# A second staging buffer for layer 0's weights, and nine bias tiles instead of ten

## The chip, the cores and the metric

The kernel runs on one core of a Trainium2 chip. The metric is the device time of one execution, in microseconds (us); the median of the runs counts. A core has TensorE (matmuls, with a queue of its own for weight loads, PEld in the profile), VectorE (DVE), ScalarE (ACT), GpSimd (POOL) and SyncE (SP), which here only issues DMAs. Each engine runs its instructions in the order of its queue; an instruction that waits holds up all that stand behind it on that engine.

## What is computed

Attention with a learned position bias, and two feed-forward layers on its output. With four batches, eight heads, 576 positions and head width 64 (2304 tokens of width 512; the hidden width of the layers is 2048):

```python
scores = scale * np.matmul(q, k.transpose(0, 1, 3, 2))
x = (psi_rel / psi_i)[..., None]
bias = np.maximum(x @ w1 + b1, 0.0) @ w2
scores = scores + bias.transpose(2, 0, 1)[None]
attn = softmax(scores)
x = (attn @ v).transpose(0, 2, 1, 3).reshape(2304, 512)
h = x @ w_in0                        # layer 0
x = (h * np.cos(h)) @ w_out0
h = x @ w_in1                        # layer 1
out = (np.maximum(h, 0) + alpha * np.minimum(h, 0)) @ w_out1
```

The feed-forward weights come in double precision; the kernel reads them as pairs of 32-bit words. Every operand of a large matmul is split into a high and a low part, and three products stand for one.

## The kernel before

**Stages.** `bias_phase` builds the bias rows in DRAM (36 groups of 16 positions). Then `attention` goes through 16 pairs of two heads and one batch: the bias belongs to the heads, so four pairs (the four batches) share one set of rows, and pair n uses set n // 4. `h_phase0` and `o_phase(0)` are layer 0, `h_phase1` and `o_phase(1)` layer 1. TensorE's part of layer 0 begins while the last pair still ends.

**A pair of attention.** Each pair has five score stages: stage 0 for the last 64 positions of both heads, stages 1 to 4 for 128 positions of each head. From pair 4 on they go in the order 1, 0, 2, 3, 4. For a stage TensorE makes the scores S (line 476), VectorE adds the bias and takes the extreme in one instruction (line 492: `P` from `S` and the bias tile `bt`, and `nm`), and ScalarE takes the exp (line 505). Then TensorE transposes the result (T_A, T_B, L_A, L_B, Tr; ScalarE and VectorE copy them out of PSUM, lines 555 and 557), GpSimd spreads the reciprocal sums (rb, line 517) and TensorE multiplies with v into x_A and x_B (lines 592, 595). The result xe goes to DRAM on SP's queue (line 613). Queries and keys of later pairs are loaded on SP and split by GpSimd (qh, kh, ql, kl; lines 454, 459).

**Bias tiles.** `load_bias` (lines 414 to 427) loads one tile of 128 x 576 for each of the nine (stage, head) parts of a set, on SP. The tiles come from the ring `bt_p` with BTB = 10 tiles. The load for the next set is written right behind the maximum of the set's last pair that reads the old part: in pairs 3, 7 and 11. A tile can be loaded once the maximum that reads its former content is done.

**Staging.** While attention runs, the weights of layer 0 are prepared piece by piece. `conv` turns a double-precision block into single precision: two ScalarE instructions (`wc`, `wp`, lines 225 and 226), two on VectorE (lines 231 and 232) and an add on GpSimd (line 235). `wi` then splits a block of w_in into a high part (a copy, GpSimd, line 314) and a low part (GpSimd, line 318). The first NDIR = 6 blocks stay on the chip; the ten others go into a tile with the tag `st` and from there to DRAM (line 321, SP, 512 KB). `stage_wo` does the same for pairs of blocks of w_out: sums and differences on VectorE (`wt`, tag `ct`, line 278), then `leave_w` for each of four groups: split by ScalarE (line 251) and GpSimd (line 253) into a tile of the tag `st` (named `sw`), and stores on SP (line 268, 256 KB each; one for the first group, two for the others). Five such pairs, k = 3 to 7, are staged in this way, the others in `h_phase0` without a store. `h_phase0` loads the staged weights back on SP. The tags `st` and `ct` belong to the pool `wt`, which has one buffer for each tag: a new `st` or `sw` tile can only be written when the store of the last one has landed.

**Order.** The order in which each engine runs all this is set by the Tile scheduler at build time, which places instructions by priority and by its own simulated times; stores and loads on SP are placed in the same way. On the chip every queue then keeps its order. The pieces of staging are written between the stages by `step`.

Of the kernel before, what the change touches and what calls it, by code (L numbers as in the profile page):

```python
# [10 lines left out]
F32R = mybir.dt.float32r  # L11
# [25 lines left out]
HP, LP, XP, CPRI, SP = 200, 0, 300, -50, 400  # L37
HIA, LOP = 2, 1
UPB, EPB = {"D": 11, "A": 4}, 6
PBUF, BTB = 6, 10  # L40
FIRST, SIDE, SMOD, BFIRST, BRATE, SPL, WS0, WSR, PER = 4, 6, 2, 8, 2.5, 3, 28, 3.2, 1.0
SR = 2.0
NSP = 2
# [29 lines left out]
def attn_mlp_kernel(ctx: ExitStack, tc: tile.TileContext, a: dict, out: bass.AP):  # L73
# [95 lines left out]
    wpool = {}  # L169
# [7 lines left out]
    cstack = ExitStack()  # L177
    rstack = ExitStack()
    astack = ExitStack()
    raws_w = {}  # L180
    pinned = []
    anchor = []
# [75 lines left out]
    def leave_w(layer, k, g, x):  # L258
        ps = GRPS[layer][g]
        n = len(ps)  # L260
        if (layer == 0 and k < NIP) or (layer == 1 and g < 3):
            w = WO[layer, g]
            yield from split_to(w[:, :, k, 0, :], w[:, :, k, 1, :], x)
            return
        st = wpool["t"].tile([128, 2, 2, 256], F32R, tag="st", name=f"sw{layer}_{k}_{g}")
        yield from split_to(st[:, 0:n, 0, :], st[:, 0:n, 1, :], x)
        for i, p in enumerate(ps):
            (ge if pinned else sy).dma_start(out=w2_d[layer][SLOT[p], :, k], in_=st[:, i].bitcast(F32))
        yield
# [31 lines left out]
    def wi(layer, f):  # L301
        box = []
        yield from conv(layer, f, 0, box)
        if layer:
            t = wt[f] = wpool["h"][(f + 1) % 4].tile([128, 2, 512], F32R, tag="w", name=f"v{f}")
        elif f < NDIR:
            t = wt[f] = wpool["a"].tile([128, 2, 512], F32R, tag="w", name=f"w{f}")
        else:
            t = wpool["t"].tile([128, 2, 2, 256], F32R, tag="st", name=f"st{f}").rearrange("p a b c -> p a (b c)")
        hi, lo = t[:, 0], t[:, 1]  # L310
        if layer:
            se.activation(out=hi, in_=box[0], func=AF.Copy)
        elif HIA == 2:
            keep(0, ge.tensor_copy(out=hi, in_=box[0]))
        else:
            keep(0, se.activation(out=hi, in_=box[0], func=AF.Copy))
        yield
        keep(1, (ve if layer else ge).tensor_tensor(out=lo, in0=box[0], in1=hi.bitcast(F32), op=ALU.subtract))
        yield
        if not layer and f >= NDIR:  # L320
            sy.dma_start(out=w_d[f], in_=t.bitcast(F32))
            yield
# [28 lines left out]
    def attention():  # L351
        with ExitStack() as c:
# [308 lines left out]
            def more_bias(g):  # L661
                nonlocal ng
                while ng < min(g, NG):
# [8 lines left out]
                    if ng == NG:  # L672
                        for _ in side:
                            pass
                        bstack.close()
                        right = dict(side="right", reuse_waits="tile")
                        wpool["s"] = rstack.enter_context(tc.tile_pool(name="ws", bufs=2, **right))
                        wpool["c"] = rstack.enter_context(tc.tile_pool(name="wc", bufs=2, **right))
                        wpool["t"] = astack.enter_context(tc.tile_pool(name="wt", bufs=1, **right))
                        wpool["a"] = astack.enter_context(tc.tile_pool(name="wa", bufs=NDIR, **right))  # L680
                        wpool["x"] = astack.enter_context(tc.tile_pool(name="xh0", bufs=NCC, **right))

            pend_exp = []
            fill = []
# [8 lines left out]
            while i < NS or pend_exp or waiting or fill:  # L693
                new = []
                if i < NS:
# [3 lines left out]
                    hp, b = pairs[n]  # L699
                    more_bias(max(BFIRST + int(BRATE * j), GNEED[s]))  # L700
                    for m in range(FIRST, NP):
                        f = pos[m, 1]
# [36 lines left out]
                else:  # L739
                    while fill and credit > 0:  # L740
                        d, fn, _ = fill.pop(0)
# [339 lines left out]
    def h_phase1():  # L1081
        runs = [[(0, 512), (512, 1024)], [(1024, 1536), (1536, 2048)], [(2048, 2304)]]
        with ExitStack() as c:
# [83 lines left out]
            step(1000)  # L1167

    attention()
    pinned.append(1)  # L1170
    h_phase0()
    astack.close()
# [70 lines left out]
```

## Time and profile before

| | us |
|---|---|
| median of three runs | 1102.74 |
| the three runs | 1100.99, 1102.74, 1106.53 |
| the profiled execution | 1098.82 |
| its span, first to last instruction | 1097.0 |
| TensorE busy | 1061.3 (97%) |
| VectorE busy | 807.9 (74%) |
| ScalarE busy | 643.9 (59%) |
| GpSimd busy | 254.4 (23%) |

The profile belongs to one execution. It gives the busy time of each engine, and each instruction's start, duration and the idle time of its engine before it, with what ended that idle time. Times in it count from the span's start. The end of a matmul is modelled from the next one's start, so that a TensorE that is shown as busy may still have waited for some tenths of a microsecond. The granted clock of TensorE is at its higher level (2.4 GHz) from 150 us on. The shares are means over stages with different limits: the bias rows until some 100 us, attention until 340, layer 0 until 713, layer 1 from there.

### The profile page before, as it was taken

The page shows a single profiled execution, that of the slowest core. Times are in us where ns is not written, and L with a number is a line of the kernel's source. Part 1 is how long each engine was busy: PE and PEld are TensorE (multiplying, and loading weights), DVE is VectorE, ACT ScalarE, POOL GpSimd, SP SyncE. Part 2 cuts the span into 40 slices and gives each one's busy share as a digit, 9 for nine tenths or more (in the row PEclk, how much of TensorE's full clock was granted, in tenths as well). Part 3 has the DMA queues.
Part 4 walks back from the last instruction along what each step waited for, and adds up shares of the span by engine and source line. Part 5 has one row for each costly group of instructions (what it writes and reads, how often), then busy time and mean ns, then how long its engine had stood idle before and what let it go on. Part 6 is the DMA issues. An engine that isn't in the chain of part 4 may idle for free.

```text
span 1097.0 us, 18821 instructions
## 1 busy us (share of the span) xinstructions
PE 1061.3 (97%) x7078; PEld 898.6 (82%) x7078; DVE 807.9 (74%) x1292; ACT 643.9 (59%) x1076; POOL 254.4 (23%) x248
## 2 busy tenths in 40 slices
PE   7689899999989999999999999999999999999998
PEld 2246677777767779888899999988888889999998
DVE  8886688777875888778787778668765847777673
ACT  6897688877885565545454454456555534444442
POOL 5405566756442220010000000423322300000000
PEclk9899999999999999999999999999999999999999
DMA  8765657666459673436568172876765649564621
GB/s 277 221 182 167 207 147 246 224 204 223 161 190 341 237 276 127 142 135 220 200 205 308 57 240 78 325 256 222 227 216 184 204 176 353 171 201 131 216 70 47
DMA packets 107595, 219.77 MB, mean 200 GB/s; under 512 B 11504, under 2 KB 57328, under 8 KB 106096
## 3 DMA queue, kind: packets, MB, share of 16 engines
q1 hardware_dynamic: 77104, 157.74, 45.1%
q10 hardware_dynamic: 27968, 50.34, 12.3%
q0 software_dynamic: 2432, 10.49, 2.5%
q8 instruction: 56, 0.92, 0.3%
q14 instruction: 35, 0.29, 0.1%
HBM read 133.98 MB, written 84.56 MB: 199 GB/s over the span
## 4 chain that ended last, share of the span: by engine, by line
PE 74%; DVE 6%; DMA 6%; ACT 3%; issue 2%; POOL 2%; SPq 0%; ACTq 0%; POOLq 0%; DVEq 0%
PE v L1138 18%; PE ob L1007 14%; PE h L804 10%; PE oc L1007 9%; PE oa L1007 9%; PE S L476 5%; PE x_B L595 2%; PE T_B L570 2%; PE T_A L570 2%; PE x_A L595 1%; DMA w_d<-sw 1%; DMA w<-w_d 1%; DMA xlo<-x_d 1%; DVE P L492 1%; DVE tb L815 1%
## 5 line engine op out<-in xcount | busy, mean ns | idle before, releaser
L1138 PE MATMUL v<-x,v 128*128 128x512 f32 (+1 forms) x984 | 198.0, 364 | 0.0
L1138 PEld LDWEIGHTS v<-x,v 128*128 128x128 f32 x984 | 168.5, 189 | 29.5
L804 PE MATMUL h<-xhi,w 128*128 128x512 f32 (+1 forms) x640 | 184.6, 372 | 0.8 <-PE h L804 0.4
L235 POOL TENSOR_TENSOR wc<-wc,wp 128x512 int32<-128x512 int32 x64 | 88.5, 1383 | 222.7 <-DVE wc L232 160.1
L804 PEld LDWEIGHTS h<-xhi,w 128*128 128x128 f32 x640 | 115.9, 188 | 24.1 <-PE h L804 1.9
L989 ACT ACTIVATE op<-a 128x768 fp32r<-128x768 f32 x84 | 70.5, 844 | 83.4 <-PE ob L1007 27.6
L804 PE MATMUL h<-xlo,w 128*128 128x512 f32 (+1 forms) x320 | 118.6, 371 | 0.0
L990 DVE TENSOR_TENSOR op<-a,op 128x768 fp32r<-128x768 f32 x84 | 80.1, 957 | 51.3 <-ACT op L989 49.1
L505 ACT ACTIVATE P<-P,nm 128x576 f32<-128x576 f32 x128 | 98.6, 772 | 21.7 <-DVE nm L492 21.5
L492 DVE CUSTOM_DVE_ANT_0 P<-S,bt 128x576 f32<-128x576 f32 x128 | 91.6, 751 | 24.6 <-PE S L476 16.6
L989 ACT ACTIVATE op<-b 128x768 fp32r<-128x768 f32 x84 | 70.7, 844 | 61.1 <-PE ob L1007 22.2
L990 DVE TENSOR_TENSOR op<-b,op 128x768 fp32r<-128x768 f32 x84 | 79.8, 955 | 27.4 <-ACT op L989 27.2
L1149 DVE SCALAR_TENSOR_TENSOR u<-v,asg,u 128x1024 f32<-128x1024 f32 (+2 forms) x48 | 48.0, 1013 | 41.2 <-ACT u L1148 40.9
L1007 PE MATMUL ob<-op,wo 128*128 128x384 f32 x432 | 76.4, 336 | 0.0
L1007 PEld LDWEIGHTS ob<-op,wo 128*128 128x128 f32 x432 | 75.1, 188 | 0.0
L804 PEld LDWEIGHTS h<-xlo,w 128*128 128x128 f32 x320 | 60.3, 189 | 10.9
L813 ACT ACTIVATE ta<-h,quart 128x1024 int32<-128x1024 f32 x36 | 39.9, 1109 | 48.2 <-PE h L804 27.4
L1148 ACT ACTIVATE u<-v,sgn 128x1024 f32<-128x1024 f32 (+2 forms) x48 | 43.0, 898 | 41.9 <-PE v L1138 41.8
L476 PE MATMUL S<-kh,qh 64*128 64x288 f32 (+1 forms) x270 | 53.4, 350 | 13.1 <-DVE nm L492 13.0
L814 DVE SCALAR_TENSOR_TENSOR tb<-ta,h 128x1024 f32<-128x1024 int32 x36 | 43.8, 1218 | 23.6 <-ACT ta L813 20.8
L817 ACT ACTIVATE tb<-tb,hpi 128x1024 f32<-128x1024 f32 x36 | 41.2, 1146 | 26.3 <-DVE tb L815 26.3
L136 DVE TENSOR_SCALAR u<-at,thr 128x576 f32<-128x576 f32 (+17 forms) x120 | 54.3, 522 | 2.1 <-PE bps L141 2.0
(154 smaller groups left out, 2142.6 us busy)
## 6 DMA issues: line engine op xcount, KB each, us to landing
a<-g_d SPq DMA_DIRECT2D x60, 384.0 KB, 4.7
g_d<-tb ACTq DMA_DIRECT2D x36, 512.0 KB, 3.2
b<-g_d SPq DMA_DIRECT2D x48, 384.0 KB, 4.6
raw<-in_wi_dram SPq DMA_DIRECT2D x32, 512.0 KB, 3.8
raw<-in_wo_dram SPq DMA_DIRECT2D x32, 512.0 KB, 3.9
g_d<-u ACTq DMA_DIRECT2D x28, 512.0 KB, 2.7
bias_d<-be SPq DMA_DIRECT2D x36, 295.5 KB, 3.5
w_d<-sw SPq DMA_DIRECT2D x35, 256.0 KB, 2.6
```

The costliest lines, as they stand in the source:

```text
L136: ve.tensor_scalar(u[:, 0:n], at[:, 0:n], thr[:, m:m + 1], None, op0=ALU.max)
L235: ge.tensor_tensor(out=c, in0=c, in1=p, op=ALU.add)
L476: pe(te.matmul(ps[:, hf, 0:HS], lhsT=w[r, 128 * i:128 * i + 128], rhs=m[r, c0:c0 + HS], start=(j == 0), stop=(j == len(terms) - 1)))
L492: keep(2, ve.tensor_tensor_reduce(out=sn.rearrange("p (a b) -> p a b", a=2), in0=ps[:, :, 0:HS], in1=bt[hp, s].rearrange("p (a b) -> p a b ...
L505: exps.append(se.activation(out=e, in_=e, func=AF.Exp, bias=nm, scale=-1.0, accum_out=sums[n, u][:, col, 0:1]))
L570: pe(te.transpose(out=ps[:, o:o + 128], in_=Pp[n, i][:, (S + 64) * h + 128 * cc:(S + 64) * h + 128 * cc + 128], identity=ident))
L804: te.matmul(ps[:, i], lhsT=w_[:, wx, w], rhs=xx[:, 0:n], start=(j == 0), stop=(j == 11))
L989: se.activation(out=o[:, 0], in_=x, func=AF.Copy)
L990: lows.append(ve.tensor_tensor(out=o[:, 1], in0=x, in1=o[:, 0].bitcast(F32), op=ALU.subtract))
L1007: ins = te.matmul(ps[:, m], lhsT=x[:, sl] if L else w[:, sl], rhs=w if L else x, start=first, stop=kk == NK - 1 and n == 2, skip_group_che ...
L1138: ins = te.matmul(both[:, i, 0:a1 - a0], lhsT=w[:, wx, 128 * cc:128 * cc + 128], rhs=x[:, xx, cc, a0 - o:a1 - o], start=(n == 0), stop=(n ...
L1149: ve.scalar_tensor_tensor(out=g, in0=ps, scalar=asg[:, f:f + 1], in1=g, op0=ALU.mult, op1=ALU.max)
```

## The change

The ring of bias tiles gets nine tiles instead of ten: as many as one set has parts, so that each part of the next set goes into a tile of which the same set still needs one. The tag `st` of layer 0 moves into a pool of its own, `wst`, with two buffers, opened behind the others on the right side and closed when `attention` has been written, before the pools of `h_phase0` are opened. `ct` stays in the old pool; layer 1's staging uses the old pool as before.

```diff
-PBUF, BTB = 6, 10
+PBUF, BTB = 6, 9
...
     astack = ExitStack()
+    sstack = ExitStack()
...
-        st = wpool["t"].tile([128, 2, 2, 256], F32R, tag="st", name=f"sw{layer}_{k}_{g}")
+        st = wpool["t" if pinned else "st"].tile([128, 2, 2, 256], F32R, tag="st", name=f"sw{layer}_{k}_{g}")
...
-            t = wpool["t"].tile([128, 2, 2, 256], F32R, tag="st", name=f"st{f}").rearrange("p a b c -> p a (b c)")
+            t = wpool["st"].tile([128, 2, 2, 256], F32R, tag="st", name=f"st{f}").rearrange("p a b c -> p a (b c)")
...
                         wpool["x"] = astack.enter_context(tc.tile_pool(name="xh0", bufs=NCC, **right))
+                        wpool["st"] = sstack.enter_context(tc.tile_pool(name="wst", bufs=2, **right))
...
     attention()
+    sstack.close()
     pinned.append(1)
```

No instruction of an engine is added or removed. TensorE's order stays but for two matmuls of layer 0. On the other engines the staging pieces move against those of attention. (Lines of the kernel after are one to three higher.)

GpSimd where pair 7 ends and pair 8 begins; stN is block N of w_in, rbN_A the spread sums of pair N. Before:

```order
L517 COPY rb6_B_2461<-sm6_B_2458 128x320
L459 TENSOR_TENSOR kl10_3050<-rk10_2914,kh10_3049 128x640
L318 TENSOR_TENSOR st7_2180<-wc0_7_0_2171,st7_2180 128x512
L789 TENSOR_TENSOR xlo0_1_4850<-xlo0_1_4850,xhi0_1_4859 128x512
L517 COPY rb7_A_2613<-sm7_A_2610 128x256
L314 CAST st8_2313<-wc0_8_0_2233 128x512
L235 TENSOR_TENSOR wc0_9_0_2378<-wc0_9_0_2378,wp0_9_0_2379 128x512
L454 CAST qh11_3297<-rq11_3169 128x640
L318 TENSOR_TENSOR st8_2313<-wc0_8_0_2233,st8_2313 128x512
```

After:

```order
L319 TENSOR_TENSOR st7_2183<-wc0_7_0_2174,st7_2183 128x512
L236 TENSOR_TENSOR wc0_8_0_2236<-wc0_8_0_2236,wp0_8_0_2237 128x512
L518 COPY rb6_B_2464<-sm6_B_2461 128x320
L460 TENSOR_TENSOR ql10_3050<-rq10_2916,qh10_3049 128x640
L460 TENSOR_TENSOR kl10_3053<-rk10_2917,kh10_3052 128x640
L791 TENSOR_TENSOR xlo0_1_4854<-xlo0_1_4854,xhi0_1_4863 128x512
L315 CAST st8_2316<-wc0_8_0_2236 128x512
L236 TENSOR_TENSOR wc0_9_0_2381<-wc0_9_0_2381,wp0_9_0_2382 128x512
L518 COPY rb7_A_2616<-sm7_A_2613 128x256
L319 TENSOR_TENSOR st8_2316<-wc0_8_0_2236,st8_2316 128x512
L315 CAST st9_2390<-wc0_9_0_2381 128x512
```

Block 7 is finished before pair 6's sums are spread instead of behind them, and block 9 is begun before pair 11's queries are split.

ScalarE in pair 13, from its first exp to the two of stage 2 (P13_1); sw0_k_g is group g of the k-th pair of w_out blocks. Before:

```order
L505 ACTIVATE P13_0_4007,sume3_119<-P13_0_4007,nm13_1_4008 128x576
L555 ACTIVATE T12_B_4026<-Tr12_4027 128x8x64
L505 ACTIVATE P13_0_4007,sume3_119<-P13_0_4007,nm13_5_4010 128x576
L555 ACTIVATE T12_B_4026<-T12_B_1_4062 128x2x256
L251 ACTIVATE sw0_3_1_3206<-wt0_3_3161 128x2x256
L225 ACTIVATE wc0_8_1_3343<-raw0_8_1_3091 128x512
L505 ACTIVATE Pr13_4058,sume4_120<-Pr13_4058,nm13_0_4059 128x576
L555 ACTIVATE T12_B_4026<-T12_B_3_4074 128x2x256
L505 ACTIVATE P13_1_4102,sume3_119<-P13_1_4102,nm13_2_4103 128x576
L505 ACTIVATE P13_1_4102,sume3_119<-P13_1_4102,nm13_6_4105 128x576
```

After:

```order
L506 ACTIVATE P13_0_4010,sume3_119<-P13_0_4010,nm13_1_4011 128x576
L227 ACTIVATE wp0_10_1_3685<-raw0_10_1_3414 128x512
L506 ACTIVATE P13_0_4010,sume3_119<-P13_0_4010,nm13_5_4013 128x576
L556 ACTIVATE T12_B_4029<-T12_B_1_4065 128x2x256
L506 ACTIVATE Pr13_4061,sume4_120<-Pr13_4061,nm13_0_4062 128x576
L556 ACTIVATE T12_B_4029<-T12_B_3_4077 128x2x256
L252 ACTIVATE sw0_4_1_3522<-wt0_4_3459 128x2x256
L226 ACTIVATE wc0_10_1_3684<-raw0_10_1_3414 128x512
L252 ACTIVATE sw0_4_2_3559<-wt0_4_3459 128x2x256
L506 ACTIVATE P13_1_4105,sume3_119<-P13_1_4105,nm13_2_4106 128x576
L506 ACTIVATE P13_1_4105,sume3_119<-P13_1_4105,nm13_6_4108 128x576
```

The staging is one pair of blocks further on at the same place, two groups are split one right behind the other, and in the whole of pair 13 ScalarE has 6 conversions and 6 splits instead of 3 and 3 (4 and 4 instead of 4 and 1 in pair 12, 5 and 5 instead of 3 and 4 in pair 14). From pair 15's first exp on, up to the last copy of a transposed tile, 5 conversions and splits remain instead of 10.

SP where the set of pairs 8 to 11 is loaded; btS_p is part p of set S. Before:

```order
L426 DMA bt1_4_1631<-bias_d_57 128x576
L433 DMA rq7_2136<-in_q_dram 128x640
L423 DMA bt1_8_1633<-bias_d_57 128x512
L424 DMA bt1_8_1633<-bias_d_57 128x64
L426 DMA bt2_1_2453<-bias_d_57 128x576
```

After:

```order
L322 DMA w_d_78<-st6_2073 128x1024
L190 DMA raw0_10_0_2385<-in_wi1_dram 128x1024
L427 DMA bt2_1_2456<-bias_d_57 128x576
L424 DMA bt2_5_2458<-bias_d_57 128x512
L425 DMA bt2_5_2458<-bias_d_57 128x64
L614 DMA x_d_58<-xe6_A_2487 128x256
L419 DMA bt2_0_2507<-bias_d_57 64x576
L322 DMA w_d_78<-st7_2183 128x1024
L419 DMA bt2_0_2507<-bias_d_57 64x576
```

The first part of a set moves from behind the last part of the set before (three pairs earlier) to the others of its own set; the store of block 7 now stands between two halves of a bias tile.

## Rows read from the trace of the kernel before

**Rows 1.** The page, part 1: busy us (share of the span) and instructions of each engine.

```profile
PE 1061.3 (97%) x7078; PEld 898.6 (82%) x7078; DVE 807.9 (74%) x1292; ACT 643.9 (59%) x1076; POOL 254.4 (23%) x248
```

**Rows 2.** Windows by pair: start:end, length, busy us (instructions) by engine, PEclk, DMA share, GB/s.

```profile
133.06:148.79 15.73, 15.64 (x145) 12.10 (x144) 12.33 (x32) 12.29 (x27) 11.73 (x13) 1.00 0.64 185
...
180.21:197.40 17.19, 16.37 (x145) 12.17 (x143) 11.38 (x31) 13.52 (x33) 12.08 (x13) 1.00 0.98 319
...
228.80:244.17 15.37, 15.37 (x143) 12.09 (x143) 12.47 (x33) 12.31 (x29) 6.70 (x8) 1.00 0.65 214
244.17:261.71 17.54, 16.38 (x144) 12.18 (x143) 11.31 (x31) 13.65 (x33) 13.11 (x14) 1.00 0.91 304
261.71:277.08 15.37, 15.37 (x143) 12.09 (x143) 13.29 (x34) 12.50 (x30) 8.10 (x9) 1.00 0.36 117
277.08:294.63 17.55, 16.14 (x145) 12.11 (x143) 14.04 (x36) 15.25 (x36) 6.60 (x8) 1.00 0.53 180
294.63:312.08 17.45, 15.73 (x143) 12.13 (x143) 13.24 (x36) 14.35 (x33) 7.45 (x8) 1.00 0.49 160
312.08:339.88 27.80, 26.02 (x199) 19.42 (x198) 17.16 (x39) 19.01 (x43) 11.73 (x12) 1.00 0.69 219
```

**Rows 3.** Waits, 120 to 340 us: in total, times, the longest.

```profile
POOL st L314 <- DMA w_d<-st: 19.5, 7, 5.1
...
ACT sw L251 <- DMA w_d<-sw: 9.1, 6, 3.9
```

**Rows 4.** Timeline of GpSimd: start, us, what [idle before it and what ended it].

```profile
192.17 0.62 POOL L314 CAST st<-wc 128x512 fp32r<-128x512 f32 x1 [5.11 <-DMA w_d<-st]
192.75 1.29 POOL L235 TENSOR_TENSOR wc<-wc,wp 128x512 int32<-128x512 int32 x1
```

**Rows 5.** Timeline of ScalarE, pair 7 and the end of attention.

```profile
194.07 0.69 ACT L226 ACTIVATE wp<-raw 128x512 int32<-128x512 uint32 x1 [1.02 <-POOL wc L235]
194.66 0.76 ACT L505 ACTIVATE P<-P,nm 128x576 f32<-128x576 f32 x1
...
320.37 0.63 ACT L251 ACTIVATE sw<-wt 128x512 fp32r<-128x512 f32 x1 [0.65 <-DMA w_d<-sw]
```

**Rows 6.** Timeline of SP's queue, stores of st.

```profile
174.82 0.37 SPq L321 DMA_DIRECT2D w_d<-st  x1
...
186.38 0.38 SPq L321 DMA_DIRECT2D w_d<-st  x1
```

**Rows 7.** Timeline of TensorE, four of its gaps.

```profile
197.40 0.37 PE L476 MATMUL S<-kh,qh 128*128 128x288 f32 x1 [0.65 <-DVE nm L492]
...
321.54 0.81 PE L592 MATMUL x_B<-T_B,v 128*128 128x320 f32 x2 [1.07 <-ACT T_B L555]
...
373.91 0.47 PE L804 MATMUL h<-xhi,w 128*128 128x512 f32 x1 [0.36 <-PE h L804]
...
396.88 0.47 PE L804 MATMUL h<-xhi,w 128*128 128x512 f32 x1 [0.32 <-DVE tb L818]
```

**Rows 8.** ScalarE's groups by form, 197.4 to 312.1 us: count, busy us, mean ns, idle before.

```profile
L225 ACT ACTIVATE wc<-raw 128x512 f32<-128x512 f32 x11 | 7.4, 673 | 0.0
...
L251 ACT ACTIVATE sw<-wt 128x512 fp32r<-128x512 f32 x4 | 2.5, 632 | 1.1 <-DMA w_d<-sw 1.0
...
L251 ACT ACTIVATE sw<-wc 128x256 fp32r<-128x256 f32 x2 | 0.8, 401 | 0.0
```

**Rows 9.** Tile bt: landing of its loads.

```profile
DMA to landing us min/median/max: 2.5/4.1/5.4
```

**Rows 10.** Tile wc (duration ns min/median/max), then VectorE and GpSimd at 281 us.

```profile
L231 DVE TENSOR_SCALAR wc<-wc x23: 421/427/1477, 129.0 to 340.9; 128x512 int32<-128x512 int32 x23
...
281.02 0.98 DVE L231 TENSOR_SCALAR wc<-wc 128x512 int32<-128x512 int32 x1 [0.65 <-ACT wc L225]
...
280.43 1.28 POOL L253 TENSOR_TENSOR sw<-wt,sw 128x512 fp32r<-128x512 f32 x1 [2.62 <-ACT sw L251]
```

**Rows 11.** Tile sw: landing of its stores.

```profile
DMA to landing us min/median/max: 2.0/2.7/9.9
```

## The prediction

> **What bounds the kernel now.** I read the page first. TensorE is busy for 1061.3 us of a span of 1097.0 [rows 1], so only some 36 us of the span can be won without taking work away, and a change to staging can only win TensorE's gaps. Then I cut the attention's steady part into windows, one for each pair of heads and batch: each begins where TensorE starts the quarter-height score matmul of stage 0 of that pair, which runs once in a pair; pair 4 starts at 133.06, pair 15 at 312.08 [rows 2]. In a window in which TensorE never waits, a pair takes 15.37 us, with TensorE busy for all of it (pair 10, pair 12). Five windows are to be looked at: pairs 7 and 11 take 17.19 and 17.54, pairs 13 and 14 take 17.55 and 17.45, and the end from pair 15's start to 339.88 holds 27.80 - 26.02 = 1.78 us without TensorE. The other six windows are one stretch of three from 133.06 to 180.21 and one of three from 197.40 to 244.17, together 93.92 us, 15.65 each.
>
> What do the slow windows wait for? The waits, engine by engine, show the one staging buffer twice: GpSimd's copy into `st` waited seven times for the store of the tile before, 19.5 us in all, and ScalarE's copy into `sw` six times, 9.1 us in all [rows 3]. Pair 7 shows how such a wait reaches TensorE. The store of the buffer is issued at 186.38, behind bias rows on SP's queue [rows 6]; GpSimd sits 5.11 us until it has landed, and its add into `wc` at 192.75 stands behind the copy [rows 4]; ScalarE's `wp` waits 1.02 us for that add, and an exp of attention stands behind `wp` at 194.66 [rows 5]; TensorE then lacks a maximum and stands still for 0.65 us at 197.40 [rows 7]. Not all of a slow window shows as a gap, since matmul ends are modelled; so I count windows, not gaps. The end shows the same by ScalarE: its copy at 320.37 waits 0.65 us for a store, T_B is copied behind it, and TensorE waits 1.07 us at 321.54 [rows 5, 7].
>
> **What the change does, part by part.** It removes no instruction and adds none, except that issues may be cut differently; the order of matmuls stays, apart from two. It moves staging work forward and removes a wait.
>
> *First, the hand-overs (pairs 7 and 11).* With two tiles GpSimd's copy waits for the store before last; here that one was issued at 174.82, 11.6 us before the store at 186.38 [rows 6], and the longest wait for a store of `st` was 5.11 us. I take the two windows to fall to the mean of the calm ones: 17.19 + 17.54 - 2 x 15.65 = 3.4 us won. The ends: nothing, if another wait takes its place, and 3.99 us, if they fall to 15.37.
>
> *Second, pairs 12 to 14.* Staging that lay behind the end of attention now lies in them, as the order of ScalarE shows. I count ScalarE's instructions per pair in both orders, from one pair's first exp to the next one's. Attention alone: pair 10 is busy for 12.31 us [rows 2] with three conversions of 0.67 us [rows 8], so 10.3 us are attention. Before, pairs 12, 13 and 14 hold 4, 3 and 3 conversions, and 1, 3 and 4 splits, two of them small: 10 x 0.67 + 6 x 0.63 + 2 x 0.40 + 3 x 10.3 = 42.2 us; the windows show 12.50 + 15.25 + 14.35 = 42.1 [rows 2, 8], so counting works. Now they hold 4, 6 and 5 conversions, and 4, 6 and 5 splits, three of them small: 15 x 0.67 + 12 x 0.63 + 3 x 0.40 + 30.9 = 49.7 us. That is 16.6 a pair, above the 15.37 that TensorE needs: ScalarE becomes the bound here. The store waits go, but the room for them goes as well. From below: when instructions stand back to back their records overlap by some 0.1 us, so a queue that never waits could need about 2.6 us less, 47.1, and 50.37 - 47.1 = 3.3 us would be won. From above: the three windows leave ScalarE idle for 50.37 - 42.1 = 8.3 us now; were it idle as long again, they would take 58.0 and lose 7.6 us. I take 17.5 us for each, by the nearest rows, the two windows that already hold such staging (17.55 and 17.45): 52.5, a loss of 2.1 us. VectorE, at 13.2 to 14.0 us in these windows, has little room either.
>
> *Third, the end of attention.* From pair 15's start there are now 5 staging pieces on ScalarE instead of 10, and none waits for the store just issued. Of TensorE's 1.78 us I take 1.5 as won; the ends are 0 and 1.78.
>
> *Fourth, after attention.* The conversions and splits that ran between 340 and 400 now lie before; with them VectorE's integer steps leave. TensorE's two gaps there, 0.36 us and 0.32 us, the second behind VectorE's tb [rows 7], should shrink; I take 0.7 us (both) as the upper end and 0.5 as the value. The loads of the staged weights wait, as before, for the last staging store ahead of them on SP; that store comes some us after the last exps in both orders, so I cost it at nothing; the cover is that layer 0's first units use the six tiles that lie on the chip.
>
> *Fifth, nine bias tiles.* The first row of the next head pair was loaded up to a pair ahead; now it waits for the same row of the last pair to be read. SP may then stand for a stage with a staging store, queries and values behind it; GpSimd, which waited for such a store at once, has the second tile, and the queries are for a pair several stages on. A row takes 2.5 to 5.4 us to land, 4.1 in the median [rows 9], and is read one window (15.37 us) later, which covers it: nothing, with 5.4 - 4.1 = 1.3 us for each of three hand-overs, 3.9 us, as the bad end. Without that cover, each late row would stop VectorE's maximum and so TensorE.
>
> *Sum.* -3.4 + 2.1 - 1.5 - 0.5 = -3.3 us. The profiled execution took 1098.8 us; it comes to 1095.5. The median of the runs shown lies 3.9 us above that execution, so the forecast for a median is 1102.7 - 3.3 = **1099.4 us**, 0.3% less. Half a per cent, 5.5 us, is about what a measurement of this kernel can tell from no change.
>
> **The rivals.**
>
> *A. The queues stay without waits.* Pairs 12 to 14 take 47.1 us. Then -3.4 - 3.3 - 1.5 - 0.5 = -8.7: 1094.0. For it: ScalarE's waits for stores are the longest single ones at the end, and a full engine finds its inputs ready. Against: VectorE and ScalarE wait for each other within a conversion.
>
> *B. Slower: ScalarE jams in pairs 12 to 14.* Its queue keeps the idle share that pair 14 has now, (17.45 - 14.35) / 17.45 = 0.178 [rows 2]; 49.7 us then need 60.5, a loss of 10.1 against 5.4 won: +4.7, 1107.4. It decides from 50.37 + 5.4 = 55.8 us on for the three windows; below that the change wins. For it: staging steps stand among the exps in a fixed order, each waiting for VectorE or GpSimd. Against: part of the idle share was waiting for stores.
>
> *C. GpSimd holds up VectorE.* VectorE's shift of `wc` takes 0.427 us in the median but up to 1.477; the one at 281.02 took 0.98 and ended just after GpSimd's split, which began at 280.43 and took 1.28 [rows 10]. With more GpSimd work in a pair, such meetings become more frequent. Eight shifts in pairs 12 to 14, each 1.05 us longer, ahead of a maximum: 8.4 us on top of the forecast, +5.1, 1107.8. Against: the median shows that most shifts meet nothing. The Trainium skill, page "SBUF — State Buffer", section "Who interferes with whom", has a rule for it: VectorE and GpSimd share a pair of ports under an exclusive lock, and the loser blocks. The trace agrees in the row at 281.02; by that rule alone the time would be 1107.8, by the median row 1099.4.
>
> *D. The change does not do what it says.* The stores land so late that two tiles do not suffice: a `sw` store took up to 9.9 us to land [rows 11]. Then nothing moves: 1102.7. Against: the median landing is 2.7 us. The Trainium skill, page "DMA: Bandwidth & Descriptors", section "Issuing engines are not separate DMA queues", says that all issues run on the same 16 DMA engines and interleave, which speaks for D where bias rows and stores meet; the window of pair 7 agrees, with a DMA share of 0.98.
>
> **How the numbers follow.** Forecast 0.50, A 0.25, B 0.12, C 0.06, D 0.07. The forecast by itself spans 1096 to 1102.5. The range takes in A with 2 us for the scatter of the runs, the forecast and D, and reaches towards B: 1092 to 1106; B's upper half, C and a stray part of A are left out. Faster by over half a per cent: A and a sixth of the forecast, 0.33. Slower by it: half of B and half of C, 0.09. The rest, 0.58, is within.
>
> **What would show it.** In the waits, GpSimd's copy into `st` for its store and ScalarE's copy into `sw` should be all but gone. Windows cut in the same way should give pairs 7 and 11 below 16 us, and pairs 12 to 14 each about 17.5 with ScalarE busy for 16 or more; no VectorE maximum should wait for a bias row. Last exp to last attention matmul should hold less than 0.5 us of TensorE gaps. I am wrong if pairs 7 and 11 stay above 17 us (the wait was not the cause), if pairs 12 to 14 take under 49 or over 56 us in sum, or if the time moves by something behind 400 us, where the order is unchanged.

## The result, and the profile after

The changed kernel takes 1108.49 us in the median of eight runs (1106.3 to 1112.45), the kernel before 1101.41 us in runs beside them (1099.77 to 1106.53). The ratio is 1.0063, with a 95% interval of 1.0044 to 1.0082: slower, by some 7 us, where 3.3 us less was forecast, and outside the range.

The busy times of the whole program hardly differ from [rows 1]; part 1 of the page of the kernel after:

```profile
PE 1062.0 (96%) x7078; PEld 899.6 (81%) x7078; DVE 803.2 (72%) x1292; ACT 643.8 (58%) x1076; POOL 256.2 (23%) x248
```

The profiled execution is the longest of its kind (1112.45 us), because bias rows came late (VectorE's maximum waited 12.2 us for one between 25 and 50 us) and pair 4 began 6.75 us later; so the windows count, not the span. The windows of the kernel after, cut as [rows 2]; shown are pairs 7, 9 and 11 to 14, and the end of attention (columns as there):

```profile
187.79:203.76 15.97, 15.63 (x142) 12.06 (x143) 12.20 (x32) 13.61 (x33) 11.80 (x13) 1.00 0.99 341
...
220.07:237.39 17.32, 15.50 (x143) 12.12 (x143) 13.34 (x33) 12.12 (x28) 11.27 (x11) 1.00 0.58 181
...
253.65:269.50 15.85, 15.64 (x142) 12.07 (x143) 12.40 (x33) 13.90 (x34) 11.16 (x13) 1.00 0.98 327
269.50:288.85 19.35, 16.40 (x142) 12.06 (x143) 16.75 (x38) 15.93 (x36) 11.58 (x10) 1.00 0.70 223
288.85:308.92 20.07, 17.22 (x142) 13.41 (x143) 17.08 (x41) 16.40 (x38) 10.43 (x11) 0.91 0.58 194
308.92:326.89 17.97, 16.21 (x144) 12.15 (x143) 15.20 (x39) 14.90 (x35) 11.04 (x10) 1.00 0.71 222
326.89:354.86 27.97, 26.13 (x197) 19.25 (x198) 14.86 (x33) 17.99 (x40) 9.39 (x10) 1.00 0.68 229
```

Pairs 12 to 14 took 50.37 us and now take 57.39. Pairs 7 and 11 fell from 34.73 to 31.82 together. The other six windows from pair 4 on rose from 93.92 to 97.87, most of all pair 9, from 16.04 to 17.32; its window before:

```profile
212.76:228.80 16.04, 15.97 (x144) 12.14 (x143) 11.32 (x31) 13.22 (x32) 12.31 (x14) 1.00 0.55 174
```

The end of attention stayed (27.80, 27.97). A second profile of each kernel, further down, says the same.

The waits, 120 to 345 us, against [rows 3]; GpSimd's wait for the store of `st` has no row any more:

```profile
ACT P L506 <- DVE nm L493: 17.7, 24, 1.8
...
PE S L477 <- DVE nm L493: 9.4, 13, 1.6
...
ACT sw L252 <- DMA w_d<-sw: 1.8, 4, 0.6
```

So 28.6 us of waiting for stores became 1.8, as the change promises. But TensorE's wait for VectorE's maximum went to 9.4 us (13 times); before, 120 to 340 us, it was 5.5 us (8 times):

```profile
PE S L476 <- DVE nm L492: 5.5, 8, 1.6
```

What makes the maximum late? The groups of VectorE, first of the kernel before, 261.71 to 312.08 us (count, busy us, mean ns, idle before):

```profile
L231 DVE TENSOR_SCALAR wc<-wc 128x512 int32<-128x512 int32 x5 | 3.6, 728 | 0.8 <-ACT wc L225 0.8
...
L232 DVE SCALAR_TENSOR_TENSOR wc<-raw,wc 128x512 int32<-128x512 int32 x5 | 3.4, 685 | 0.1
```

and of the kernel after, 269.50 to 326.89 us:

```profile
L493 DVE CUSTOM_DVE_ANT_0 P<-S,bt 128x576 f32<-128x576 f32 x24 | 17.2, 748 | 1.7 <-PE S L477 1.6
L233 DVE SCALAR_TENSOR_TENSOR wc<-raw,wc 128x512 int32<-128x512 int32 x8 | 8.1, 1007 | 0.2
L232 DVE TENSOR_SCALAR wc<-wc 128x512 int32<-128x512 int32 x7 | 4.8, 682 | 1.1 <-ACT wc L226 1.0
L279 DVE TENSOR_TENSOR wt<-wc 128x256 f32<-128x256 f32 x4 | 3.2, 793 | 1.5 <-POOL wc L236 1.5
```

More steps (shifts, two-input steps and `wt`: 19 before, 31 now), and longer ones: the one that reads `raw` and `wc` took 685 ns and takes 1007. The maximum keeps its 748 ns. If I take 425 ns for an undisturbed shift, 690 for an undisturbed step with two inputs and 420 for a `wt`, all that lies above is an excess: 1.8 us in pairs 12 to 14 before, 5.9 after. ScalarE's staging pieces there (conversions and splits) are 30 in its order, before 18. Two theories remain, rivals B (ScalarE jams) and C (GpSimd holds up VectorE). One place shows both. VectorE, pair 13:

```profile
293.58 0.78 DVE L232 TENSOR_SCALAR wc<-wc 128x512 int32<-128x512 int32 x1
294.39 1.66 DVE L233 SCALAR_TENSOR_TENSOR wc<-raw,wc 128x512 int32<-128x512 int32 x1
```

GpSimd:

```profile
292.79 2.71 POOL L254 TENSOR_TENSOR sw<-wt,sw 128x512 fp32r<-128x512 f32 x2 [3.40 <-ACT sw L252]
296.13 1.27 POOL L236 TENSOR_TENSOR wc<-wc,wp 128x512 int32<-128x512 int32 x1 [0.63 <-DVE sm_A L515]
```

ScalarE, then TensorE:

```profile
297.43 0.67 ACT L227 ACTIVATE wp<-raw 128x512 int32<-128x512 uint32 x1 [1.93 <-POOL wc L236]
298.00 0.61 ACT L252 ACTIVATE sw<-wc 128x512 fp32r<-128x512 f32 x1
298.52 0.57 ACT L556 ACTIVATE T_B<-L_B 128x512 f32<-128x512 f32 x1
```

```profile
299.14 0.90 PE L593 MATMUL x_B<-T_B,v 128*128 128x320 f32 x2 [1.99 <-ACT T_B L556]
```

Two subtractions of GpSimd stand back to back; VectorE's step beside them takes 1.66 us instead of 0.69, GpSimd's add comes after it, ScalarE's `wp` waits 1.93 us for the add, T_B stands behind `wp` and a split, and TensorE waits 1.99 us.

### The profile page after: what moved, and what is told of

Its sections match the earlier page's. It is cut to its first block, busy times and chain, and to the rows that moved or that the text cites. A ratio compares the mean times of both kernels' runs of the same rounds, so it can differ in the third digit from the quotient of the medians.

```text
span 1110.7 us, 18834 instructions
## 1 busy us (share of the span) xinstructions
PE 1062.0 (96%) x7078; PEld 899.6 (81%) x7078; DVE 803.2 (72%) x1292; ACT 643.8 (58%) x1076; POOL 256.2 (23%) x248
## 4 chain that ended last, share of the span: by engine, by line
PE 73%; DVE 7%; DMA 6%; ACT 3%; issue 2%; POOL 1%; SPq 0%; ACTq 0%; POOLq 0%; DVEq 0%
PE v L1140 18%; PE ob L1009 14%; PE h L806 14%; PE oc L1009 9%; PE oa L1009 8%; PE S L477 4%; DMA w_d<-sw 2%; DVE P L493 2%; PE T_B L571 2%; PE x_B L596 2%; PE T_A L571 1%; ACT P L506 1%; DMA g_d<-tb 1%; DMA w<-w_d 1%; DVE wc L233 1%
## 5 line engine op out<-in xcount | busy, mean ns | idle before, releaser
L236 POOL TENSOR_TENSOR wc<-wc,wp 128x512 int32<-128x512 int32 x64 | 85.1, 1330 | 286.8 <-DVE wc L233 224.9
L477 PEld LDWEIGHTS S<-kh,qh 64*128 64x128 f32 (+1 forms) x270 | 29.4, 190 | 33.8 <-issue 21.2
L233 DVE SCALAR_TENSOR_TENSOR wc<-raw,wc 128x512 int32<-128x512 int32 x64 | 55.8, 875 | 1.2
```

Of the source, the lines that this page charges most:

```text
L233: hold(ve.scalar_tensor_tensor(out=c, in0=raw[:, :, 1], scalar=-2 ** 31, in1=c, op0=ALU.bitwise_and, op1=ALU.bitwise_xor))
L236: ge.tensor_tensor(out=c, in0=c, in1=p, op=ALU.add)
L477: pe(te.matmul(ps[:, hf, 0:HS], lhsT=w[r, 128 * i:128 * i + 128], rhs=m[r, c0:c0 + HS], start=(j == 0), stop=(j == len(terms) - 1)))
```

## The experiments

**The smaller ring, and the profile again.** First the ring of nine alone, on the kernel before:

```diff
-PBUF, BTB = 6, 10
+PBUF, BTB = 6, 9
```

> The kernel before with the ring of bias tiles at nine instead of ten and nothing else: one staging tile as before. Theory R (the smaller ring costs what was lost, since a bias row's load is issued later): 1106 to 1108 us, with VectorE's maximum waiting for bias rows, and windows of attention above 16 us all along. Theory J (the crowding of staging costs it): 1101.4 us within 1.5, ratio to the kernel before between 0.9985 and 1.0015, with pairs 12 to 14 at 50.4 us and pairs 7 and 11 at 34.7 together.

1101.16 us, ratio 0.9998 (0.9987 to 1.001), pairs 12 to 14 at 50.48 us: the ring costs nothing. Then the changed kernel again, unedited:

> The changed kernel a second time, unchanged. In its first profile pairs 12 to 14 took 57.39 us where the kernel before took 50.37, pairs 7 and 11 together 31.82 where it took 34.73, and pairs 8 to 10 together 49.89 where it took 46.77; that execution was also some 4 us slower than the other runs of the kernel, in which the load of the bias rows at 25 to 50 us came late. Theory J (staging is crowded into pairs 12 to 14, so ScalarE's and VectorE's queues jam there): pairs 12 to 14 again between 55.5 and 58.5 us, pairs 7 and 11 again under 33. Theory O (the first profile was an odd execution): pairs 12 to 14 under 54 us, and the span under 1103 us.

1110.24 us; pairs 12 to 14 at 58.33, pairs 7 and 11 at 31.74. The first profile was odd before pair 4 alone. The last runs held the kernel before again:

> The kernel before, unchanged, for a second profile. Its first profiled execution took 1098.82 us, 2.6 us under its median. If that was luck at the start of the program, the second shows pair 4 later than 133.06 us and pairs 12 to 14 at 50.4 us again; if pairs 12 to 14 vary by themselves, they take 51 us or more here.

1101.95 us, pair 4 at 135.62, pairs 12 to 14 at 50.53, the end of attention at 28.20. So the windows repeat to within 1 us, and the place of the loss is shown: 7.0 to 8.0 us in pairs 12 to 14, 1.0 to 1.3 in pairs 4 to 11, nothing at the end and nothing that both profiles agree on behind it (755.84 and 758.14 us after, 757.12 and 757.44 before).

**One half of the change at a time.** Two tiles for w_in alone (the pool has one buffer of each of two tags):

```diff
+ wpool["st"] = sstack.enter_context(tc.tile_pool(name="wst", bufs=1, **right))
...
- t = wpool["st"].tile([128, 2, 2, 256], F32R, tag="st", name=f"st{f}")...
+ t = wpool["st"].tile([128, 2, 2, 256], F32R, tag=("st", "su")[f % 2], name=f"st{f}")...
```

> Two staging tiles for layer 0's w_in blocks alone; the groups of w_out go through one of these two tiles, so that each of them waits for the store of the group before it, as in the kernel before. Ring of nine. ScalarE's staging pieces in pairs 12 to 14 are 6, 7 and 8 in its order, where the changed kernel has 8, 12 and 10 and the kernel before 5, 6 and 7. Theory J: the loss of pairs 12 to 14 (57.39 against 50.37) goes for the most part, to 51 to 53 us, and the time is between 1100 and 1103 us. Theory C (VectorE and GpSimd hold each other up wherever staging is no longer spaced by stores, in the w_in blocks as in the w_out groups): pairs 8 to 11 stay as slow as in the changed kernel (65.74 us against 64.31) and the time is between 1103 and 1106 us.

and for w_out alone (tag `st` for `wi`, `("st", "su")[(4 * k + g) % 2]` for `leave_w`):

> The other half: one staging tile for layer 0's w_in blocks, two for the groups of w_out. Ring of nine. ScalarE's staging pieces in pairs 12 to 14 are 5, 11 and 10 in its order, where the changed kernel has 8, 12 and 10 and the kernel before 5, 6 and 7. Theory J: most of the loss is in this half, pairs 12 to 14 take 54 to 57 us in sum, pairs 7 and 11 stay at 34 to 35 together, and the time is between 1104 and 1109 us. Theory C: less GpSimd work per pair than in the changed kernel before pair 12, so pairs 8 to 10 are back at 46.8 us, and pairs 12 to 14 lose in proportion to GpSimd's busy time there.

1134.57 us (1.0303) and 1127.21 us (1.0235): both theories missed by 18 to 32 us, for a reason that none of them held. After attention TensorE stood 27.38 and 20.11 us for layer 0's first `tb`, which the changed kernel does not do. The windows can still be read. With two tiles for w_in, pairs 4 to 11 take 129.61 us, as in the changed kernel (129.69; before 128.65): what pairs 7 and 11 win is lost there in the others. With two for w_out alone they take 128.44; in these windows both runs came out as theory C had it. Pairs 12 to 14 take 56.36 and 53.99 us. The first misses theory J, which wanted 51 to 53 for 21 pieces on ScalarE: with one tile for the groups, ScalarE again waited 3.8 us for stores there. The number of pieces is not all.

**ScalarE's load or GpSimd's subtractions.** Two edits to the changed kernel, in `split_to`, for the groups during attention: a copy in place of GpSimd's subtraction (the kernel then leaves the low part out),

```diff
- hold((eng or (ve if pinned else ge)).tensor_tensor(out=lo, in0=w, in1=hi.bitcast(F32), op=ALU.subtract))
+ if pinned:
+     hold(ve.tensor_tensor(out=lo, in0=w, in1=hi.bitcast(F32), op=ALU.subtract))
+ else:
+     hold(ge.tensor_copy(out=lo, in_=hi.bitcast(F32)))
```

> The changed kernel, but where GpSimd makes the low part of a layer 0 group during attention (a subtraction, 1.28 us for 512 columns), it copies the high part instead (a copy, 0.61 us): the low part is left out, so the result is not the reference's. GpSimd has some 0.67 us less for each of the 14 groups in pairs 12 to 14; ScalarE's staging pieces there are 28 in its order instead of 30. Theory C (GpSimd's splits stretch VectorE's staging steps that read two tiles of SBUF or shift in place; in the changed kernel's profile these steps hold 5.9 us more than undisturbed ones in pairs 12 to 14, before 1.8): the excess falls to about 3 us and pairs 12 to 14 to 53 to 55 us, the time to 1103 to 1106 us. Theory B (ScalarE's own load of staging pieces sets the pace): two pieces fewer, 1.3 us, so pairs 12 to 14 at 56 to 57.5 us and the time at 1106 to 1108 us.

or the high part on GpSimd,

```diff
- hold(se.activation(out=hi, in_=w, func=AF.Copy))
+ hold(se.activation(out=hi, in_=w, func=AF.Copy) if pinned else ge.tensor_copy(out=hi, in_=w))
```

> The changed kernel, but the high part of layer 0's w_out groups during attention is made by GpSimd (a copy, 0.61 us) instead of ScalarE (0.63 us). ScalarE's staging pieces in pairs 12 to 14 fall from 30 to 11, all of them conversions; GpSimd's rise by some 10 us. Theory B: ScalarE has room, pairs 12 to 14 fall to 47 to 51 us and the time to 1099 to 1103 us. Theory C: more GpSimd work beside VectorE's staging steps, pairs 12 to 14 stay at 55 to 59 us and the time at 1106 us or above.

or both:

> The changed kernel with both edits to the w_out groups during attention: the high part is made by GpSimd, and the low part is a copy as well (the low part is left out, so the result is not the reference's). ScalarE has 10 staging pieces in pairs 12 to 14, GpSimd's splits are two copies of 0.61 us each. One edit alone gave 53.9 us (low part a copy) and 52.9 us (high part on GpSimd) for pairs 12 to 14, where the changed kernel has 57.4 and 58.3. If the two costs (ScalarE's load, and VectorE stretched by GpSimd's subtractions) add, the sum is 48 to 50 us; if either of them alone suffices to jam the queues, it is 52 to 54 us. The time is long by the stall after attention as with the high part alone, 1115 to 1120 us.

| kernel | pairs 12 to 14 | VectorE busy there | its staging steps | their excess | ScalarE busy there | GpSimd busy there |
|---|---|---|---|---|---|---|
| before | 50.37 | 40.57 | 19 | 1.8 | 42.10 | 22.14 |
| changed (first profile) | 57.39 | 49.03 | 31 | 5.9 | 47.23 | 33.05 |
| low part a copy | 53.87 | 43.43 | 29 | 0.8 | 46.50 | 22.89 |
| high part on GpSimd | 52.92 | 43.77 | 22 | 3.8 | 39.09 | 29.98 |
| both | 48.98 | 42.07 | 22 | 2.1 | 38.82 | 23.06 |

With the copy ScalarE is as busy as before the edit, within 0.7 us, and 3.5 us are gone; the time is 1103.24 us, 1.0018 (1.0002 to 1.0034), as theory C said (the excess fell further than its 3 us). VectorE's groups, 265.44 to 319.31 us, show shorter steps:

```profile
L233 DVE SCALAR_TENSOR_TENSOR wc<-raw,wc 128x512 int32<-128x512 int32 x7 | 5.6, 796 | 0.1
L232 DVE TENSOR_SCALAR wc<-wc 128x512 int32<-128x512 int32 x7 | 3.0, 425 | 2.2 <-ACT wc L226 2.1
...
L282 DVE TENSOR_TENSOR wt<-wc 128x256 f32<-128x256 f32 x3 | 1.3, 419 | 0.0
```

The edit also takes 10.2 us of work off GpSimd, so GpSimd's shorter queue may have a share in the 3.5 us; no run tells the two apart.

With the high part on GpSimd 4.5 us are gone: less than theory B wanted, and more than theory C's nothing. Both edits win 8.4 us, the sum of 3.5 and 4.5 within 0.4. So the loss has two parts that add, one that goes with GpSimd's subtractions and one that goes with the splits on ScalarE. But the new order also puts fewer staging steps into these windows, 22 of VectorE's instead of 31, so the 4.5 us are not shown to be ScalarE's splits alone; a pair of runs with equal steps comes at the end of this section. (The second and the third edit took 1121.07 and 1118.46 us in all, with a stall of TensorE after attention of 18.1 and 18.9 us.) The last of this group keeps GpSimd's time for each group and changes the kind of instruction:

```diff
+ for _ in range(2):
+     hold(ge.tensor_copy(out=lo, in_=hi.bitcast(F32)))
```

> The changed kernel, with two copies of the high part (0.61 us each) on GpSimd in place of the subtraction (1.28 us): the low part is left out, so the result is not the reference's. GpSimd's time per group is as in the changed kernel, only the kind of instruction differs; ScalarE has 23 staging pieces in pairs 12 to 14. Theory C by kind (a subtraction reads two tiles of SBUF and stretches VectorE's steps, a copy hardly does): VectorE's excess in pairs 12 to 14 is under 2.5 us (5.9 in the changed kernel) and the three pairs take 50 to 53.5 us. If GpSimd's time alone counts: 55 to 57 us, as with w_in's two tiles alone (56.4 us with 21 pieces). Layer 0 stalls as with the other variants that leave more groups behind, some 1115 to 1125 us in all.

1124.60 us; the excess is 1.3 us, as by kind, but the three pairs take 54.43 us, between the two forecasts: ScalarE waited 3.4 us for stores in them and TensorE 2.22 and 3.40 us for T_B. Fewer groups fell into these windows as well (23 of VectorE's steps, GpSimd busy for 24.08 us instead of 33.05). So the run shows that VectorE's steps stay short beside copies, and does not tell the kind of GpSimd's work from its amount.

**Pace, and the stall behind attention.** The changed kernel with fewer staging steps in a stage:

```diff
-SR = 2.0
+SR = 1.5
```

> The changed kernel with the pace of staging, SR, at 1.5 steps a stage instead of 2: both tiles stay, but ScalarE's staging pieces in pairs 12 to 14 are 9, 5 and 5 in its order (19; 30 in the changed kernel, 18 in the kernel before), and more groups are left for the time after attention (19 instead of 12, before 20). Theory J (crowding in pairs 12 to 14 is the loss, whether by ScalarE or GpSimd): pairs 12 to 14 at 49 to 52 us, pairs 4 to 11 as in the changed kernel (129.7 us), and 1098 to 1102 us. Theory L (what is left for the time after attention stops layer 0, as when only one kind of staging had two tiles, where TensorE stood 20 to 27 us for VectorE's tb): 1115 us or more.

> The same with SR at 1.2: ScalarE's staging pieces in pairs 12 to 14 are 2, 5 and 3 in its order, 10 in all, and 24 groups are left for the time after attention. Theory J: pairs 12 to 14 at 47 to 49 us, and 1096 to 1100 us if what is left behind attention costs nothing. Theory L: 1115 us or more, and more than with SR at 1.5.

1126.98 and 1145.01 us. Pairs 12 to 14 fall to 51.15 and 47.32 us, so the crowding there is gone, though at SR 1.5 pairs 4 to 11 rise to 132.85 (129.69 in the changed kernel); and the stall comes instead: TensorE at SR 1.2,

```profile
395.60 0.79 PE L806 MATMUL h<-xhi,w 128*128 128x512 f32 x1 [47.65 <-DVE tb L820]
```

and ScalarE at that time, the last splits and the first `ta`:

```profile
380.08 1.15 ACT L252 ACTIVATE sw<-wt 128x512 fp32r<-128x512 f32 x2 [3.03 <-DVE wt L279]
386.45 0.63 ACT L252 ACTIVATE sw<-wc 128x512 fp32r<-128x512 f32 x1 [5.22 <-DMA w_d<-sw]
386.99 1.10 ACT L815 ACTIVATE ta<-h,quart 128x1024 int32<-128x1024 f32 x1
```

In these kernels `ta` stands behind the last left-over split; in the kernel before it stands among them, and in the changed kernel so few are left that it hardly matters. The tile of `ta` is allocated once the new pool is closed. My reading was that it lies in that pool's memory and so waits for its last store. The test puts one tile back into the old pool, which stays open, and sends the left-overs through that one:

```diff
+ def turn():
+     turns.append(1)
+     return "st" if len(turns) % 2 and not tails_on else "t"
...
- t = wpool["st"].tile(...)
+ t = wpool[turn()].tile(...)
...
+ tails_on.append(1)
  step(1000)
```

> Two tiles in two pools: tile A with tag st in the old pool, which stays open through layer 0's first phase, tile B in the new pool, which is closed with attention. While attention's stages are written they alternate; what is left behind the last stage goes through A alone. Pace SR 1.5, ring of nine. In this order layer 0's first ta (ScalarE) stands ahead of the left-over splits, where with both tiles in the new pool it stands behind the last of them. Theory M (layer 0's tiles lie in the memory that the new pool gives back, and so wait for its last store; that is the 18 to 48 us stall of TensorE): the stall goes, and the time is 1098 to 1104 us, against 1126.98 with the same pace and both tiles in the new pool. Theory L (whatever is left behind attention stops layer 0): 1115 us or more.

> The same with SR at 1.2, where with both tiles in the new pool it took 1145.01 us. Theory M: 1096 to 1102 us, with pairs 12 to 14 at 47 to 49 us. Theory L: 1125 us or more. A third possibility: the groups of w_out left behind attention (24) now compete with layer 0's first units on VectorE and ScalarE, then 1102 to 1110 us with TensorE's gaps between 345 and 430 us.

> The kernel before (one tile, ring of ten) with SR at 1.2 alone: it tells what of the last run is due to the pace and what to the second tile. If the second tile is what helps, it is slower than the last run by about 3 us, with GpSimd's and ScalarE's waits for stores in it; if the pace is what helps, the two agree within 1.5 us.

1106.15 us (1.0044, 1.0025 to 1.0062) and 1101.58 us (0.9993, 0.9976 to 1.0011): the long stalls are gone (4.1 and 4.9 us of TensorE's waits for `tb` are left), and the times 20.8 and 43.4 us shorter than with the same pace in one pool. SR 1.5 missed its forecast by 2 us; its windows of pairs 5, 10 and 13 took 17.6 to 18.0 us. That the pool sets the order is shown; that it does so through the memory is argued, as the addresses were not read. With one tile and SR 1.2: 1102.0 us (1.0001, 0.9985 to 1.0017). The two agree, so the second tile brings nothing at this pace. The slower pace wins nothing by itself either: with one tile attention ends 3.8 us earlier than in the kernel before, and between 340 and 720 us TensorE then waits 6.5 us for `tb` (0.3 before).

**A version that beats both.** ScalarE's splits cost, and GpSimd's queue, as I read it, holds little that attention waits for. So the high part goes to GpSimd in the kernel before, with its one tile and ring of ten (the edit is that of the high part above), and in the kernel with two tiles in two pools at SR 1.5:

> The kernel before (one tile, ring of ten), with the high part of layer 0's w_out groups during attention made by GpSimd instead of ScalarE. The wait for the store then holds up GpSimd and no longer ScalarE, and ScalarE loses 8 of its 18 staging pieces in pairs 12 to 14. Theory B: pairs 13 and 14 fall from 17.5 to 15.4 to 16.5 us each and the waits of TensorE for T_B at 304 and 321 us go; the time is 1096 to 1099 us. Theory C: GpSimd's longer queue stretches VectorE's steps, nothing is won: 1101 to 1104 us.

> Two tiles in two pools as in the run with SR 1.5 (1106.15 us), with the high part of the w_out groups on GpSimd. If the second tile is worth its hand-overs once ScalarE is relieved: 1096 to 1099 us, below the run with one tile. If VectorE's meetings with GpSimd eat it up (Theory C): 1101 to 1106 us, no better than with one tile.

1096.36 us (0.9946, 0.9926 to 0.9966) and 1096.23 us (0.9948, 0.993 to 0.9966): both faster than the kernel before, and equal. The second differs from the kernel with SR 1.5 and two pools (ratio 1.0044) in the engine of the splits alone. Its pairs 12 to 14 took 51.12 us with the splits on ScalarE and take 48.20 with them on GpSimd:

```profile
sum 51.12, PE 47.97 PEld 36.33 DVE 42.01 ACT 42.76 POOL 23.20; mean PE 15.99 PEld 12.11 DVE 14.00 ACT 14.25 POOL 7.73
sum 48.20, PE 47.36 PEld 36.40 DVE 42.30 ACT 39.27 POOL 29.60; mean PE 15.79 PEld 12.13 DVE 14.10 ACT 13.09 POOL 9.87
```

VectorE has 22 staging steps there in both, and their excess does not fall (2.0 and 2.4 us). So 2.9 us are won by the move of the splits, without fewer steps of VectorE. The first once more, for a second profile:

> One tile, ring of ten, high part of the groups on GpSimd, a second time: 1095 to 1098.5 us, ratio to the kernel before 0.993 to 0.997. In the windows, pairs 13 and 14 together 33 to 34.5 us (35.0 in the kernel before) and pair 15's start to the last x_B 25 to 26 us (27.8 before).

1098.07 us, 0.9965 (0.995 to 0.998). Its pairs 13, 14 and the end of attention:

```profile
277.68:295.58 17.90, 15.66 (x145) 12.22 (x143) 13.74 (x35) 12.61 (x30) 8.23 (x11) 1.00 0.49 154
295.58:311.78 16.20, 15.58 (x145) 12.12 (x143) 14.16 (x36) 13.38 (x31) 8.10 (x11) 1.00 0.50 165
311.78:337.28 25.50, 25.50 (x199) 19.44 (x198) 14.87 (x35) 16.38 (x37) 10.67 (x12) 1.00 0.62 211
```

The end of attention went from 27.80 to 25.50 without a gap of TensorE, pair 14 from 17.45 to 16.20; pair 13 did not fall, against theory B's forecast. The first profile has 25.56, 16.23 and 18.01. The waits for the stores did not go. In the first profile of this kernel, 120 to 340 us, they are longer than in [rows 3]:

```profile
POOL st L314 <- DMA w_d<-st: 21.8, 7, 5.7
...
POOL sw L251 <- DMA w_d<-sw: 18.7, 8, 3.9
```

In the second profile these rows have 17.7 and 17.6 us. They are GpSimd's now, and none is ScalarE's.

## Why the prediction was wrong

*Hand-overs (-3.4 forecast).* Pairs 7 and 11 gave 2.9 us, and the waits went as said. But pairs 6 and 8 to 10 gave 4.0 us back, which the sum did not hold. In pair 9 of the changed kernel VectorE's two-input step meets GpSimd's copies of queries and keys; VectorE, GpSimd, TensorE:

```profile
232.05 1.09 DVE L233 SCALAR_TENSOR_TENSOR wc<-raw,wc 128x512 int32<-128x512 int32 x1
233.06 0.74 DVE L493 CUSTOM_DVE_ANT_0 P<-S,bt 128x576 f32<-128x576 f32 x1
```

```profile
231.67 0.92 POOL L455 CAST qh<-rq 128x640 fp32r<-128x640 f32 x1 [3.46 <-PE S L477]
232.54 1.18 POOL L455 CAST kh<-rk 128x640 fp32r<-128x640 f32 x1
```

```profile
234.64 0.40 PE L477 MATMUL S<-kh,qh 64*128 64x288 f32 x2 [1.03 <-DVE nm L493]
```

In pairs 6 and 10 it is a shift beside GpSimd's subtraction into `st`, 1.45 and 1.46 us instead of 0.42; the maxima follow it on VectorE, and TensorE waits 0.50 and 0.51 us, where these windows had no gap before. Pair 6, VectorE, GpSimd, TensorE:

```profile
183.84 1.45 DVE L232 TENSOR_SCALAR wc<-wc 128x512 int32<-128x512 int32 x1
183.72 1.29 POOL L319 TENSOR_TENSOR st<-wc,st 128x512 fp32r<-128x512 f32 x1
187.79 0.37 PE L477 MATMUL S<-kh,qh 128*128 128x288 f32 x1 [0.50 <-DVE nm L493]
```

The step I got wrong here was to treat the six calm windows as fixed.

*Pairs 12 to 14 (+2.1 forecast).* This is the step that failed. The place and the sign were right, and ScalarE's count was near (49.7 us counted, 47.1 at its lower end, 47.23 busy). The size, 52.5, came from the two windows that already held such staging; measured are 57.39 and 58.33, at the upper end that I gave (58.0) and past rival B's point of 55.8, from which the change loses. The rows I took it from hold three or four splits, not four to six, and the cost does not stay the same per window: VectorE's busy time went from 40.57 to 49.03 us, to which I gave one sentence and no price. Nor did ScalarE become the bound, as I had it: it stood idle for 57.39 - 47.23 = 10.16 us in these windows, and for 8.27 before. What I had wrong is the wait of the engines for each other, not ScalarE's load.

*Rivals B and C.* Each explained a part, and I priced them as alternatives, at 0.12 and 0.06. The runs show both at work, and adding: 3.5 us went with GpSimd's subtractions, and 4.5 with the splits moved off ScalarE, fewer steps of VectorE included (2.9 in the pair of runs with equal steps). How the 7 us divide exactly stays open. That B's 1107.4 and C's 1107.8 lie near 1108.49 is luck: both count on 5.4 us won outside pairs 12 to 14, where the windows lost 1.2. Against C stood "the median shows that most shifts meet nothing". A median over all 23 shifts was the wrong number: it is that of a step which meets nothing, and the change raises the number of meetings. By overlap of the rows, 11 of the 23 shifts met a GpSimd instruction before, 18 of 24 after; of the two-input steps 6 of 23 and 11 of 24.

*End of attention (-1.5), after it (-0.5).* Nothing came: 27.80 to 27.97 us, and no change behind it that both profiles share. The wait for the store at the end is gone, but TensorE's idle time there is 27.97 - 26.13 = 1.84 us, where it was 1.78: four gaps of 0.20 to 0.77 us, for VectorE or ScalarE, took its place. *Nine bias tiles (0).* Right. *Rival A* is excluded, and so is *D*: the waits are gone.

## What to carry to other kernels

A wait is worth removing on the engine whose queue something critical stands in: 28.6 us of waiting went from GpSimd and ScalarE and the kernel lost 7 us, while the best version waits longer for the same stores, on GpSimd alone, and wins 3.8 to 5.9. A buffer that stalls producers also paces them: before widening it, count on every engine what then arrives in the tightest windows, and for VectorE count at the durations that its steps have beside GpSimd, not at the median. And look at what else a new pool's lifetime orders: closed with left-over staging still in it, it went with a stall of 18 to 48 us in seven of these kernels.

## What had not been expected of the hardware

VectorE's staging steps by what GpSimd did at the same time, from the rows of nineteen profiles of these kernels, 130 to 345 us (count, median us, longest; an overlap from 0.1 us on counts):

| VectorE step | GpSimd idle | beside a copy | beside an add or subtraction |
|---|---|---|---|
| shift of `wc`, 128x512 | 181, 0.42, 0.43 | 78, 0.51, 0.91 | 172, 0.72, 1.73 |
| `wc` from `raw` and `wc`, 128x512 | 279, 0.69, 0.72 | 81, 0.77, 1.18 | 72, 1.22, 1.92 |
| `wt`, 128x256 | 234, 0.42, 0.43 | 41, 0.49, 0.80 | 35, 0.93, 1.54 |

Without GpSimd these steps hardly vary; beside an add or a subtraction (1.28 us alone) one takes up to 1.3 us longer, as long as GpSimd's instruction. The maximum, which reads scores from PSUM, takes 0.75 us in both cases. The rule of the Trainium skill, page "SBUF — State Buffer", section "Who interferes with whom", says which steps can meet GpSimd: a VectorE instruction with two SBUF inputs contends with a GpSimd instruction that reads SBUF, and one with at most one such input, outside the two-port modes, does not. The trace agrees, 0.69 to 1.22 us in the median for the step of `raw` and `wc` and 0.75 unchanged for the maximum. The shift has one SBUF input and is stretched too (0.42 to 0.72); by this rule it would have to run in a two-port mode, and no run here shows its mode. The page also has it that whoever issues first holds the ports and the other blocks. Here GpSimd is held up as well, but by less: its copy of keys, 0.72 us in the median, took 1.18 in the row at 232.54, and its subtraction of 128x512, 1.28 us alone, at most 1.82.

TensorE's granted clock was 0.91 in the window of pair 13 of the changed kernel and 1.00 in all its other windows shown. Cut finer, that window shows the gap of 1.99 us and the clock behind it (columns as in [rows 2]):

```profile
297.00:299.00 2.00, 0.16 (x2) 0.00 (x0) 1.57 (x4) 1.57 (x4) 0.99 (x3) 1.00 0.88 151
299.00:301.00 2.00, 1.86 (x8) 1.60 (x9) 1.52 (x5) 2.00 (x7) 1.02 (x1) 0.68 0.97 378
301.00:303.00 2.00, 2.00 (x14) 1.67 (x14) 1.75 (x3) 1.55 (x4) 0.79 (x1) 0.50 0.93 345
303.00:305.00 2.00, 2.00 (x22) 1.21 (x18) 1.57 (x5) 0.77 (x2) 1.65 (x2) 0.96 0.36 131
```

TensorE stood still for nearly all of 297 to 299 us, and from 301 to 303 the clock was at its lower level (0.50, 1.2 GHz). In the second profile the same pair took 20.75 us at a clock of 1.00, so the clock is not what made the window long.
